# One hand-written order for the attention steps of a fused attention and two-stage MoE kernel

## The chip, the cores and the metric

The kernel runs on one core of a Trainium2 chip. TensorE (PE) multiplies, VectorE (DVE) and ScalarE (ACT) work element by element, GpSimd (POOL) fills constants, and the sync engine's queue (SP) issues nearly all DMAs; ACT's queue issues the rest. Matmul results go to eight PSUM banks. The metric is the device time of one execution, in microseconds; of several runs the median counts.

## The reference

Linear attention without a softmax, an RMS norm over each head, then two feed-forward stages, all in fp32:

```python
kv  = einsum('bhsd,bhse->bhde', k, v)          # b=4, h=8, s=576, d=64
out = einsum('bhsd,bhde->bhse', q, kv)
x   = out / sqrt(mean(out*out, -1) + 1e-6) * g_norm      # -> [2304, 512]
h   = x @ w_in;  x = (h * clip(h + 3, 0, 6) / 6) @ w_out # d_ff = 2048
p   = domain_probs / (domain_probs.sum(-1) + 1e-9)
y   = sum_e p[:, e] * (relu(x @ w1[e]) @ w2[e])          # 4 experts, 1024 wide
```

## The kernel before

**Attention** is done in eight half batches i (a batch, four of its eight heads). For each: `att_q` transposes q on PE into banks `pq` and `kvp` by matmuls with an identity, and ACT copies them out as `qT` (L225 from `pq`, L227 from `kvp`); `att_kv` sums k-transposed times v into `kvp`, and ACT copies the 64x64 blocks into the block-diagonal `kvbd` (L242); `att_out` multiplies `qT` with `kvbd` into three banks `po`, called groups 0, 1 and 2 (2 is half size), whose squares ACT writes to `xt` (L261) and DVE sums (`ssq`, L264); `att_rms` makes 1/rms in small DVE steps around an ACT square root (L287) and scales `po` into `xt` (L277); `att_x` transposes `xt` on PE into three banks `px` (two long pieces 0 and 1, a short piece 2), from which ACT writes `xh` (L323) and DVE the rest `xl` (L324). Each pair `xh`, `xl` holds one fp32 value as two parts that TensorE takes at its faster format.

**Weights** are split in the same way: `convert` turns a raw tile, in two halves, by some ACT steps (L149, L150, L165) and seven DVE steps (L152 to L167) into `w`. `conv(k)` runs k of its pieces.

**The first MoE** works in units u of feature tiles f, over five token blocks t. `ff_in` is 12 matmuls (L342 to L344) into `ph` and an epilogue on ACT and DVE (L348 to L351); `ff_out` is 12 matmuls (L365) into four banks. `step(n)` does `ff_in` of item n, `ff_out` of item n-3 and some conversion. The four items of `EARLY` (unit 0, blocks 0 and 1) have their `ff_in` pulled into the end of attention by `fill`. **The second MoE** (L646, L692) follows and isn't touched.

**The order.** The code is written by loop step: step i issues `att_q`, `att_kv` of i, `att_out` and `att_rms` of i-1 and `att_x` of i-2. A scheduler of the framework then reorders the instructions of all engines by priority and readiness in its own model, so what stands on an engine isn't the order of the code. Each engine runs its own list strictly from the front.

Of the kernel before, what the change touches and what calls it, by code (L numbers as in the profile page):

```python
# [17 lines left out]
def kernel(  # L18
# [63 lines left out]
    psb = ctx.enter_context(tc.tile_pool(name="psb", bufs=5, space=bass.MemoryType.PSUM))  # L82
    psc = ctx.enter_context(tc.tile_pool(name="psc", bufs=1, space=bass.MemoryType.PSUM))
# [23 lines left out]
    ssq = const.tile([P, 5, HH], F32, name="ssq")  # L107
    xH = [(xp0 if t < 3 else xp).tile([P, KD, n], F32R, tag=f"xh{t}", name=f"xh{t}") for t, (_, n) in enumerate(BLK)]
# [68 lines left out]
    def att_load(i):  # L177
        b, hf = divmod(i, 2)
        t = {}
        for nm, src in (("q", q), ("k", k), ("v", v)):  # L180
            m = natile[0] % 7
            natile[0] += 1
            pool, tag = (accp, "acc") if m < 5 else (wp, f"w{m - 1}")
            t[nm] = pool.tile([P, NP, CJ, D], F32, tag=tag, name=f"{nm}in")
            nc.sync.dma_start(
                out=t[nm].rearrange("p r j d -> p r (j d)"),
                in_=src[b, hf * HH:(hf + 1) * HH].rearrange("(r x) (s j) d -> (x s) r (j d)", x=2, j=CJ),
            )
# [21 lines left out]

    def att_q(i):

        t = st[i]
# [4 lines left out]
        for j in range(CJ):
            for x in range(2):
                for r in range(NP):  # L220
                    to = pq[r][half[x ^ r], j, :] if j < CB else kvp[r][half[x ^ r], 1, :]
# [4 lines left out]
        for r in range(NP):
            nc.scalar.activation(out=qv[:, r, :, CB], in_=kvp[r][:, 1, :], func=AF.Copy)  # L227

    def att_kv(i):


        t = st[i]
        kvp = t["kvp"]
        for j in range(CJ):
            for x in range(2):
                for r in range(NP):
                    nc.tensor.matmul(  # L237
                        kvp[r][half[x ^ r], 0, :], lhsT=t["k"][half[x], r, j, :], rhs=t["v"][half[x], r, j, :],
                        start=(j == 0), stop=(j == CJ - 1))
        for r in range(NP):  # L240
            for x in range(2):
                nc.scalar.activation(  # L242
                    out=kvbd[i % 2][half[x ^ r], r, half[x]], in_=kvp[r][half[x ^ r], 0, :], func=AF.Copy)

    def att_out(i):
# [3 lines left out]
        t["xt"] = xt = wp.tile([P, 3, 2, HH, D], F32, tag=f"w{2 + i % 2}", name="xt")  # L249
        t["po"] = []  # L250
        for tt in banks(b):
            po = psb.tile([P, 2, NP, P], F32, tag="b", name="po")
            for m, (o, w) in enumerate(tt):
                for r in range(NP):
                    nc.tensor.matmul(  # L255
                        po[:w, m, r, :], lhsT=t["qT"][:, r, o:o + w], rhs=kvbd[i % 2][:, r, :],
                        start=True, stop=True)
            t["po"].append(po)
        for g, tt in enumerate(banks(b)):
            w, nm = tt[0][1], len(tt)  # L260
            nc.scalar.activation(  # L261
                out=xt[:w, g, :nm].rearrange("p m h d -> p m (h d)"),
                in_=t["po"][g][:w, :nm].rearrange("p m r e -> p m (r e)"), func=AF.Square)
            nc.vector.tensor_reduce(  # L264
                out=ssq[:w, 2 * g:2 * g + nm, :], in_=xt[:w, g, :nm], axis=AX.X, op=ALU.add)

    def att_rms(i):


        b, hf = divmod(i, 2)  # L270
        t = st[i]
        va, r0, w1_, ri = (sp.tile([P, 5, HH], F32, tag=n, name=n) for n in ("va", "r0", "nw", "ri"))

        def scale():
            for g, tt in enumerate(banks(b)):
                w, nm = tt[0][1], len(tt)
                nc.vector.tensor_tensor(  # L277
                    out=t["xt"][:w, g, :nm].rearrange("p m h d -> p (m h) d"),
                    in0=t["po"][g][:w, :nm].rearrange("p m r (h d) -> p (m r h) d", d=D),
                    in1=ri[:w, 2 * g:2 * g + nm, :].rearrange("p m h -> p (m h)").unsqueeze(2).to_broadcast(  # L280
                        [w, nm * HH, D]),
                    op=ALU.mult)

        return [
            lambda: nc.vector.tensor_scalar(
                out=va, in0=ssq, scalar1=1.0 / D, scalar2=1e-6, op0=ALU.mult, op1=ALU.add),
            lambda: nc.scalar.activation(out=r0, in_=va, func=AF.Sqrt),  # L287
            lambda: nc.vector.reciprocal(out=r0, in_=r0),
            lambda: nc.vector.scalar_tensor_tensor(
                out=w1_, in0=va, scalar=FMAX, in1=r0, op0=ALU.min, op1=ALU.mult),  # L290
            lambda: nc.vector.tensor_tensor(out=w1_, in0=w1_, in1=r0, op=ALU.mult),
            lambda: nc.vector.tensor_scalar(
                out=w1_, in0=w1_, scalar1=-0.5, scalar2=1.5, op0=ALU.mult, op1=ALU.add),
            lambda: nc.vector.tensor_tensor(out=ri, in0=w1_, in1=r0, op=ALU.mult),
            scale,
        ]

    def att_x(i):

        b, hf = divmod(i, 2)  # L300
        t = st.pop(i)
        where = {o: (g, m, w) for g, tt in enumerate(banks(b)) for m, (o, w) in enumerate(tt)}
        c = cut(b)
        long, short = ((0, c), (c, S)) if c > S - c else ((c, S), (0, c))
        em = []

        def bank(rs, o0, o1):
            px = bank_a([P, len(rs), o1 - o0], "px")
            for y, r in enumerate(rs):
                for o in sorted(where):  # L310
                    g, m, w = where[o]
                    if o0 <= o < o1:
                        nc.tensor.transpose(  # L313
                            px[:, y, o - o0:o - o0 + w],
                            t["xt"][:w, g, m, 2 * r:2 * r + 2, :].rearrange("p h d -> p (h d)"),
                            ident[:w, :w])
            blk, off = divmod(b * S + o0, TB)
            assert off + o1 - o0 <= BLK[blk][1]
            d = hf * NP + rs[0]
            hi = xH[blk][:, d:d + len(rs), off:off + o1 - o0]  # L320
            lo = xL[blk][:, d:d + len(rs), off:off + o1 - o0]
            em.append((
                lambda: nc.scalar.activation(out=hi, in_=px, func=AF.Copy, scale=gcol[:, 0:1]),  # L323
                lambda: nc.vector.scalar_tensor_tensor(  # L324
                    out=lo, in0=px, scalar=gcol[:, 0:1], in1=hi.bitcast(F32), op0=ALU.mult, op1=ALU.subtract)))

        for r in range(NP):
            bank([r], *long)
        bank(list(range(NP)), *short)
        return em  # L330
# [56 lines left out]
    nearly = [0]  # L387

    def fill():
        ff_in(*EARLY[nearly[0]])  # L390
        nearly[0] += 1
# [395 lines left out]
```

## Time and profile before

| what | value |
|---|---|
| median of three runs | 1234.98 us (1234.45 to 1235.54) |
| profiled execution: time, span | 1236.37 us, 1234.6 us |
| PE busy, share of the span | 1216.7 us, 99% |
| DVE, ACT busy | 759.1 us, 529.6 us |
| chain that ended last, share of PE | 96% |
| largest lines in that chain | po L646 32%, po L365 16%, qa and qb L692 14% each |
| DMA over the span | 87.14 MB, 71 GB/s |

The span runs from the first to the last instruction of the profiled execution; its own time holds 1.8 us more around it. A busy share says how long an engine had an instruction in it, not how fast that went. Times in rows are microseconds from the span's start. Matmuls of fp32 operands show two records each.

### The profile page before, as it was taken

How to read it: one execution, taken by the hardware profiler on the slowest of the kernel's cores; microseconds unless marked ns; L12 is line 12 of the kernel's file. 1: busy time of each engine (PE TensorE's matmuls, PEld its weight loads, DVE VectorE, ACT ScalarE, POOL GpSimd, SP SyncE). 2: the span in 40 equal slices, each digit the busy share in tenths (PEclk: the TensorE clock that was granted, in tenths of full speed). 3: DMA queues.
4: the chain of work that ended last, by engine and by line, in shares of the span. 5: the costliest groups of instructions: out<-in, count | busy, mean ns of one | idle time of the engine just before them, and what ended most of it. 6: DMA issues, size and time to landing. Idle time of an engine off the chain costs nothing.

```text
span 1234.6 us, 17429 instructions
## 1 busy us (share of the span) xinstructions
PE 1216.7 (99%) x7069; PEld 1067.9 (87%) x7069; DVE 759.1 (61%) x1457; ACT 529.6 (43%) x1050; POOL 1.6 (0%) x12
## 2 busy tenths in 40 slices
PE   7899999999999999999999999999999999999998
PEld 5778888888888889999999999999999999999997
DVE  6799974794533656565656595656565956565553
ACT  5667742542322433434444454333333534444441
POOL 0000000000000000000000000000000000000000
PEclk8999999999999999999999999999999999999999
DMA  9712320120010002211111131211221321122111
GB/s 337 232 68 86 104 68 1 52 69 1 19 51 1 1 1 69 68 67 65 60 66 64 62 115 67 69 68 68 69 69 69 109 79 69 69 69 68 69 35 52
DMA packets 60832, 87.14 MB, mean 71 GB/s; under 512 B 5200, under 2 KB 37968, under 8 KB 60752
## 3 DMA queue, kind: packets, MB, share of 16 engines
q1 hardware_dynamic: 60592, 86.03, 20.5%
q8 instruction: 55, 0.90, 0.3%
q14 instruction: 25, 0.20, 0.1%
q10 hardware_dynamic: 160, 0.00, 0.0%
HBM read 81.30 MB, written 4.72 MB: 70 GB/s over the span
## 4 chain that ended last, share of the span: by engine, by line
PE 96%; DMA 1%; DVE 1%; ACT 1%; issue 0%; DVEq 0%
PE po L646 32%; PE po L365 16%; PE qa L692 14%; PE qb L692 14%; PE ph L342 5%; PE ph L343 5%; PE ph L344 5%; PE po L255 1%; PE pq L222 1%; DMA qin<-in_q_dram 1%; PE px L313 1%; DMA raw<-in_moe_w_in_dram 1%; PE kvp L237 0%; DVE ssq L264 0%; PE kvp L222 0%
## 5 line engine op out<-in xcount | busy, mean ns | idle before, releaser
L646 PE MATMUL po<-wout,g 128*128 128x512 f32 x1728 | 420.3, 392 | 0.0
L646 PEld LDWEIGHTS po<-wout,g 128*128 128x128 f32 x1728 | 322.2, 188 | 61.7
L692 PE MATMUL qa<-xs,win 128*128 128x384 f32 x1008 | 203.7, 336 | 0.0
L692 PE MATMUL qb<-xs,win 128*128 128x384 f32 x1008 | 203.6, 336 | 0.0
L365 PE MATMUL po<-gH,w 128*128 128x512 f32 (+1 forms) x640 | 194.0, 369 | 0.0
L692 PEld LDWEIGHTS qa<-xs,win 128*128 128x128 f32 x1008 | 179.8, 188 | 5.7
L692 PEld LDWEIGHTS qb<-xs,win 128*128 128x128 f32 x1008 | 179.7, 188 | 5.6
L365 PEld LDWEIGHTS po<-gH,w 128*128 128x128 f32 x640 | 117.0, 188 | 20.1
L342 PE MATMUL ph<-xh,w 128*128 128x512 f32 (+1 forms) x320 | 118.1, 369 | 0.8 <-DVE xl L324 0.8
L349 DVE SCALAR_TENSOR_TENSOR r<-r,ph 128x512 f32<-128x512 f32 (+1 forms) x80 | 50.5, 632 | 111.2 <-ACT r L348 111.1
L365 PE MATMUL po<-gL,w 128*128 128x512 f32 (+1 forms) x320 | 117.8, 368 | 0.0
L343 PE MATMUL ph<-xl,w 128*128 128x512 f32 (+1 forms) x320 | 117.8, 368 | 0.0
L344 PE MATMUL ph<-xh,w 128*128 128x512 f32 (+1 forms) x320 | 117.8, 368 | 0.0
L348 ACT ACTIVATE r<-ph,three 128x512 f32<-128x512 f32 (+1 forms) x80 | 51.4, 643 | 152.4 <-PE ph L344 152.3
L666 DVE SCALAR_TENSOR_TENSOR g<-qa,g 128x384 fp32r<-128x384 f32 x48 | 26.7, 557 | 119.5 <-ACT g L665 118.2
L561 DVE TENSOR_TENSOR wout<-raw,wout 128x512 fp32r<-128x512 f32 x96 | 65.8, 687 | 28.0 <-ACT wout L560 28.0
L666 DVE SCALAR_TENSOR_TENSOR g<-qb,g 128x384 fp32r<-128x384 f32 x48 | 26.7, 557 | 89.0 <-ACT g L665 89.0
L665 ACT ACTIVATE g<-cs 128x384 fp32r<-128x384 f32 x96 | 49.7, 518 | 56.5 <-DVE cs L713 53.4
L342 PEld LDWEIGHTS ph<-xh,w 128*128 128x128 f32 x320 | 60.3, 188 | 11.5 <-DVE xl L324 1.1
L560 ACT ACTIVATE wout<-raw 128x512 fp32r<-128x512 f32 x96 | 55.4, 624 | 33.5 <-PE po L646 33.5
L344 PEld LDWEIGHTS ph<-xh,w 128*128 128x128 f32 x320 | 60.3, 188 | 10.2
L343 PEld LDWEIGHTS ph<-xl,w 128*128 128x128 f32 x320 | 60.4, 189 | 10.0
(93 smaller groups left out, 1256.8 us busy)
## 6 DMA issues: line engine op xcount, KB each, us to landing
raw<-in_moe_w_dram SPq DMA_DIRECT2D x96, 512.0 KB, 4.2
raw<-in_moe_w_in_dram SPq DMA_DIRECT2D x16, 512.0 KB, 3.7
raw<-in_moe_w_out_dram SPq DMA_DIRECT2D x16, 512.0 KB, 3.6
qin<-in_q_dram SPq DMA_DIRECT2D x8, 576.0 KB, 8.0
kin<-in_k_dram SPq DMA_DIRECT2D x8, 576.0 KB, 6.0
vin<-in_v_dram SPq DMA_DIRECT2D x8, 576.0 KB, 6.3
out_dram<-acc SPq DMA_DIRECT2D x18, 256.0 KB, 2.0
dp<-in_moe_domain_probs_dram SPq DMA_DIRECT2D x1, 36.0 KB, 6.0
```

The source lines that it names most:

```text
L342: nc.tensor.matmul(ph, lhsT=w[:, 0, c, :], rhs=xH[t][:, c, :], start=(c == 0), stop=False)
L343: nc.tensor.matmul(ph, lhsT=w[:, 0, c, :], rhs=xL[t][:, c, :], start=False, stop=False)
L344: nc.tensor.matmul(ph, lhsT=w[:, 1, c, :], rhs=xH[t][:, c, :], start=False, stop=(c == KD - 1))
L348: nc.scalar.activation(out=r, in_=ph, func=AF.Relu, bias=three[:, 0:1])
L349: nc.vector.scalar_tensor_tensor(out=r, in0=r, scalar=6.0, in1=ph, op0=ALU.min, op1=ALU.mult)
L365: nc.tensor.matmul(po_t[u, t][o], lhsT=lhsT, rhs=rhs, start=(f == 0 and m == 0), stop=(f == UF[u] - 1 and m == 2))
L560: nc.scalar.activation(out=dst[0], in_=src, func=AF.Copy)
L561: nc.vector.tensor_tensor(out=dst[1], in0=src, in1=dst[0].bitcast(F32), op=ALU.subtract)
L646: nc.tensor.matmul(ps[i], lhsT=lhsT, rhs=w[:, f, y], start=(j == 0 and f == 0 and m == 0), stop=(j == FP - 1 and f == 1 and m == 2))
L665: nc.scalar.activation(out=g[0], in_=src, func=AF.Relu)
L666: nc.vector.scalar_tensor_tensor(out=g[1], in0=src, scalar=0.0, in1=g[0].bitcast(F32), op0=ALU.max, op1=ALU.subtract)
L692: nc.tensor.matmul(bank, lhsT=w[:, wy, AOP[m], c], rhs=xs[m][:, xy, c], start=first and n == 0, stop=n == 5, skip_group_check=True)
```

## The change

Attention's work is cut into small functions (`q`, `qc`, `kv`, `kvc`, `out`, `sq`, `ssq`, `rt`, `va`, `nw`, `sc`, `x`, `hi`, `lo`), and a table `STEPS` names for each loop step which of them comes when and for which half batch (its second entry is the lag). `tc.manual_schedule()` takes the scheduler out for this part: each engine gets its instructions in the order of the table. A table `ELSE` places conversions, raw loads, the early `ff_in` items (now three pieces: matmuls, first and second half of the epilogue) and the expert probabilities at (loop step, place). `kvp`, `pq`, `px` and the early `ph` rotate over five banks instead of three, `po` over three. The square root takes `ssq` itself, with scale and bias, and the Newton step is one DVE instruction shorter. The gain vector and the probabilities are loaded at the start from ACT's queue; the loads of k and v of half batch i+2 and of q of i+3 are issued from SP's queue right behind the k-v sum of i.

```diff
-    psb = ctx.enter_context(tc.tile_pool(name="psb", bufs=5, space=bass.MemoryType.PSUM))
-    psc = ctx.enter_context(tc.tile_pool(name="psc", bufs=1, space=bass.MemoryType.PSUM))
+    psb = ctx.enter_context(tc.tile_pool(name="psb", bufs=3, space=bass.MemoryType.PSUM))
+    psc = ctx.enter_context(tc.tile_pool(name="psc", bufs=3, space=bass.MemoryType.PSUM))
...
     def bank_a(shape, name):
+        pool, tag = (psa, "a") if turn["a"] % 5 < 2 else (psc, "c")
         turn["a"] += 1
-        pool, tag = (psc, "c") if turn["a"] % 3 == 0 else (psa, "a")
...
+    def att_rt(i):
+        st[i]["r0"] = r0 = sp.tile([P, 5, HH], F32, tag="r0", name="r0")
+        nc.scalar.activation(out=r0, in_=ssq, func=AF.Sqrt, scale=1.0 / D, bias=eps[:, 0:1])
...
-    load_raw()
-    att_load(0)
-    load_raw()
-    load_raw()
...
-    att_load(1)
-    conv(6)
+    STEPS = (
+        ("kvc", 1), ("out", 1, 1), ("out", 1, 0), ("x", 2, 0), ("sq", 1, 1), ("out", 1, 2), ("sq", 1, 0),
+        ("lo", 3, 2), ("hi", 2, 0), ("sq", 1, 2), ("x", 2, 1), ("ssq", 1, 1), ("ssq", 1, 0), ("lo", 2, 0),
+        ("hi", 2, 1), ("q", 0), ("qc", 0), ("ssq", 1, 2), ("lo", 2, 1), ("rt", 1), ("kv", 0), ("va", 1),
+        ("nw", 1), ("sc", 1, 1), ("x", 2, 2), ("sc", 1, 0), ("sc", 1, 2), ("hi", 2, 2))
...
+    n = len(STEPS)
+    ELSE = {
+        (1, n): lambda: conv(3), (3, n): lambda: conv(1), (5, n): load_raw, (6, 20): lambda: conv(1),
+        (7, n): lambda: (fill(0), conv(2)),
+        (8, 9): lambda: (fill(1), fill(0)), (8, 16): lambda: conv(2), (8, 19): lambda: fill(0),
+        (8, n): lambda: (fill(2), fill(1), load_raw(), conv(2)),
+        (9, 11): lambda: fill(1), (9, 14): lambda: conv(2),
+        (9, n): lambda: (fill(3), load_raw(), fill(2), fill(2)),
+        (10, n): lambda: (fill(3), fill(3), probabilities()),
+    }
-    for i in range(NHB + 2):
-        if 1 <= i < NHB - 1:
-            att_load(i + 1)
-        if i >= NHB - 1:
-            load_raw()
-        if i == 4:
-            nc.sync.dma_start(out=dp, in_=moe2_domain_probs.rearrange("(t p) e -> p t e", p=P))
-        if i < NHB:
-            att_q(i)
-            if i == 0:
-                warm(4)
-            att_kv(i)
-        conv({0: 6, 1: 13}.get(i, 0))
...
+    with tc.manual_schedule():
...
+        nc.scalar.dma_start(out=dp, in_=moe2_domain_probs.rearrange("(t p) e -> p t e", p=P))
+        load_raw()
+        att_load(0, "q")
+        load_raw()
+        for x in ((0, "k"), (0, "v"), (1, "q"), (1, "k"), (1, "v")):
+            att_load(*x)
+        load_raw()
+        att_load(2, "q")
+
+        conv(10)
+        for i in range(NHB + 3):
+            for m, (name, lag, *part) in enumerate(STEPS):
+                if (i, m) in ELSE:
+                    ELSE[i, m]()
+                if 0 <= i - lag < NHB:
+                    DO[name](i - lag, *part)
+                if name == "kv":
+                    for x in ((i + 2, "k"), (i + 2, "v"), (i + 3, "q")):
+                        att_load(*x)
+                    if i == 0:
+                        warm(4)
+            if (i, n) in ELSE:
+                ELSE[i, n]()
+        ahead[0] = True
+        for n in range(FIRST):
+            step(n)
```

What this does to the lists of the engines, at three places. First PE in one loop step in the middle of attention, before and then changed; `pq`, `kvp` are the transposes of q and the k-v sum, `po` the product, `px` the transposes of the result.

```order
L255 MATMUL po<-kvbd_110,qT 128x128 x5
L222 MATMUL pq<-ident,qin 64x64 x32
L222 MATMUL kvp<-ident,qin 64x64 x2
L255 MATMUL po<-kvbd_110,qT 128x128 x2
L222 MATMUL kvp<-ident,qin 64x64 x2
L255 MATMUL po<-kvbd_110,qT 128x128
L237 MATMUL kvp<-vin,kin 64x64 x36
L255 MATMUL po<-kvbd_110,qT 64x128 x2
```

```order
L262 MATMUL po<-kvbd_110,qT 128x128 x8
L320 MATMUL px<-ident,xt 128x128 x3
L320 MATMUL px<-ident,xt 128x64
L262 MATMUL po<-kvbd_110,qT 64x128 x2
L320 MATMUL px<-ident,xt 128x128 x3
L320 MATMUL px<-ident,xt 128x64
L223 MATMUL pq<-ident,qin 64x64 x32
L223 MATMUL kvp<-ident,qin 64x64 x4
L243 MATMUL kvp<-vin,kin 64x64 x36
L320 MATMUL px<-ident,xt 128x128 x2
```

Before, products of the half batch ahead stand between the transposes of q and the k-v sum; now the k-v sum follows the transposes directly, and the products stand at the head of the step.

Second ACT in the same part, before and then changed; `xh` is what ACT writes from `px`.

```order
L225 ACTIVATE qT<-pq 128x64x8 x2
L227 ACTIVATE qT<-kvp 128x64 x2
L261 ACTIVATE xt<-po 128x512
L149 ACTIVATE x<-raw 128x512
L242 ACTIVATE kvbd_110<-kvp 64x64 x4
L261 ACTIVATE xt<-po 64x256
L323 ACTIVATE xh_115<-px,gcol 128x384 x2
```

```order
L232 ACTIVATE qT<-pq 128x64x8 x2
L234 ACTIVATE qT<-kvp 128x64 x2
L282 ACTIVATE r_930<-ssq,eps 128x20
L331 ACTIVATE xh_116<-px,gcol 128x2x128
L250 ACTIVATE kvbd_111<-kvp 64x64 x4
L269 ACTIVATE xt<-po 128x512 x2
L331 ACTIVATE xh_116<-px,gcol 128x384
```

The copy of the short piece (`xh_116`, 2x128) now stands ahead of the `kvbd` copies, and the conversion step (`x<-raw`) is gone from this place.

Third ACT in the changed kernel after the last half batch's products; `w` is a converted weight half, `gH` the early items' result.

```order
L269 ACTIVATE xt<-po 64x256
L331 ACTIVATE xh_117<-px,gcol 128x320
L166 ACTIVATE w<-r 128x512
L359 ACTIVATE gH<-r 128x512
L282 ACTIVATE r_1341<-ssq,eps 128x20
L331 ACTIVATE xh_118<-px,gcol 128x512
```

The weight half of feature tile 1 and the last square root stand here behind a copy from `px`; in the kernel before, that weight half is converted far ahead of this place.

## Rows read from the trace of the kernel before

**Rows 1.** Busy time by stretch; columns in its first line.

```profile
core 0: us, PE busy (x) PEld busy (x) DVE busy (x) ACT busy (x) POOL busy (x), PEclk, DMA share, GB/s
0.00:6.00 6.00, 4.82 (x12) 1.60 (x12) 1.07 (x3) 2.79 (x4) 1.62 (x12) 1.00 0.66 231
6.00:24.00 18.00, 11.05 (x305) 9.69 (x304) 11.63 (x22) 10.65 (x25) 0.00 (x0) 0.72 1.00 381
24.00:76.00 52.00, 46.91 (x1039) 39.15 (x1038) 44.37 (x116) 33.66 (x96) 0.00 (x0) 0.97 0.64 209
76.00:99.25 23.25, 22.43 (x117) 17.38 (x115) 20.37 (x48) 15.87 (x34) 0.00 (x0) 1.00 0.15 46
99.25:1234.60 1135.35, 1131.51 (x5604) 1000.11 (x5602) 681.67 (x1271) 466.60 (x896) 0.00 (x0) 1.00 0.18 59
```

**Rows 2.** Timeline of ACT and PE: start, us, engine, line, operation.

```profile
23.97 0.77 ACT L242 ACTIVATE kvbd<-kvp 64x64 f32<-64x64 f32 x4
...
39.61 0.79 ACT L242 ACTIVATE kvbd<-kvp 64x64 f32<-64x64 f32 x4 [1.04 <-PE kvp L237]
...
75.87 0.79 ACT L242 ACTIVATE kvbd<-kvp 64x64 f32<-64x64 f32 x4 [0.62 <-PE kvp L237]
...
99.25 0.40 PE L342 MATMUL ph<-xh,w 128*128 128x512 f32 x1
...
107.15 2.72 PE po L365 x12
```

**Rows 3.** Timeline, transposes of q, copies and k-v sum, PE and ACT.

```profile
24.78 1.16 PE L222 MATMUL pq<-ident,qin 64*64 64x64 f32 x64
...
26.00 1.08 ACT L225 ACTIVATE qT<-pq 128x512 f32<-128x512 f32 x2 [0.50 <-PE kvp L222]
...
66.12 0.41 ACT L227 ACTIVATE qT<-kvp 128x64 f32<-128x64 f32 x2
...
66.46 1.39 PE L237 MATMUL kvp<-vin,kin 64*64 64x64 f32 x72 [0.33 <-ACT qT L227]
...
67.89 0.79 ACT L242 ACTIVATE kvbd<-kvp 64x64 f32<-64x64 f32 x4 [0.36 <-PE kvp L237]
```

**Rows 4.** Timeline, transposes of the result, products, ACT held by a raw load, and kvbd.

```profile
39.86 1.36 PE L313 MATMUL px<-ident,xt 128*128 128x128 f32 x10
...
41.14 1.38 PE L255 MATMUL po<-kvbd,qT 128*128 128x128 f32 x10
...
50.15 0.66 ACT L149 ACTIVATE x<-raw 128x512 f32<-128x512 f32 x1 [3.44 <-DMA raw<-in_moe_w_in_dram]
...
51.27 0.78 ACT L242 ACTIVATE kvbd<-kvp 64x64 f32<-64x64 f32 x4
...
51.76 1.12 PE L313 MATMUL px<-ident,xt 128*128 128x128 f32 x6 [1.87 <-ACT kvbd L242]
```

**Rows 5.** Groups by line, first 100 us, ACT and DVE.

```profile
L323 ACT ACTIVATE xh<-px,gcol 128x384 fp32r<-128x384 f32 x6 | 3.3, 580 | 0.0
...
L323 ACT ACTIVATE xh<-px,gcol 128x128 fp32r<-128x128 f32 x2 | 0.7, 365 | 0.0
...
L277 DVE TENSOR_TENSOR xt<-po,ri 128x512 f32<-128x512 f32 x16 | 10.4, 684 | 0.2
```

**Rows 6.** Timeline at the start: ACT's conversion steps, PE's warming matmuls.

```profile
1.18 4.92 PE L450 MATMUL zp<-zero 128*128 128x512 bf16 x12 [1.18 <-DVE zero L445]
...
4.47 0.66 ACT L149 ACTIVATE x<-raw 128x512 f32<-128x512 f32 x1 [2.46 <-DMA raw<-in_moe_w_in_dram]
...
8.79 0.63 ACT L165 ACTIVATE w<-r 128x512 fp32r<-128x512 f32 x1 [1.58 <-DVE r L163]
```

**Rows 7.** Busy time by stretch, columns as in the first group.

```profile
50.00:55.00 5.00, 3.24 (x28) 2.79 (x30) 3.78 (x9) 4.45 (x13) 0.00 (x0) 0.84 1.04 395
...
55.00:60.00 5.00, 4.97 (x146) 4.46 (x143) 4.97 (x14) 3.02 (x8) 0.00 (x0) 0.82 0.49 147
```

**Rows 8.** Timeline of SP, the load behind that of the probabilities.

```profile
40.58 4.59 SPq L185 DMA_DIRECT2D qin<-in_q_dram  x1
```

**Rows 9.** Groups by line, 100 to 160 us, DVE.

```profile
L167 DVE TENSOR_TENSOR w<-r,w 128x512 fp32r<-128x512 f32 x12 | 8.2, 685 | 0.0
```

More of the change, by code (lines that the diff above doesn't have):

```diff
@@ L242, in att_kv, with att_out @@
                 nc.scalar.activation(
-                    out=kvbd[i % 2][half[x ^ r], r, half[x]], in_=kvp[r][half[x ^ r], 0, :], func=AF.Copy)
-    def att_out(i):
+                    out=kvbd[i % 2][half[x ^ r], r, half[x]], in_=st[i]["kvp"][r][half[x ^ r], 0, :], func=AF.Copy)
+    def att_out(i, g):
+        t = st[i]
+        if "po" not in t:
+            t["xt"] = wp.tile([P, 3, 2, HH, D], F32, tag=f"w{2 + i % 2}", name="xt")
+            t["po"] = {}
+        t["po"][g] = po = psb.tile([P, 2, NP, P], F32, tag="b", name="po")
+        for m, (o, w) in enumerate(banks(i // 2)[g]):
+            for r in range(NP):
+                nc.tensor.matmul(
+                    po[:w, m, r, :], lhsT=t["qT"][:, r, o:o + w], rhs=kvbd[i % 2][:, r, :],
+                    start=True, stop=True)
@@ L248, in att_out @@
         t = st[i]
[L249 to L302, printed above, removed]
         c = cut(b)
         long, short = ((0, c), (c, S)) if c > S - c else ((c, S), (0, c))
[L305 to L330, printed above, removed]
@@ new lines, in att_x @@
+        rs, (o0, o1) = ([y], long) if y < NP else (list(range(NP)), short)
+        px = bank_a([P, len(rs), o1 - o0], "px")
+        for z, r in enumerate(rs):
+            for o, g, m, w in sorted((o, g, m, w) for g, tt in enumerate(banks(b)) for m, (o, w) in enumerate(tt)):
+                if o0 <= o < o1:
+                    nc.tensor.transpose(
+                        px[:, z, o - o0:o - o0 + w],
+                        t["xt"][:w, g, m, 2 * r:2 * r + 2, :].rearrange("p h d -> p (h d)"),
+                        ident[:w, :w])
@@ L335, with ff_in @@
     po_t = {}
-    def ff_in(u, t, f):
+    def ff_in(u, t, f, bank=None):
         n = BLK[t][1]
         w = W[u, f][:, 0].rearrange("p j (c f) -> p j c f", c=KD)
-        ph = psa.tile([P, TB], F32, tag="a", name="ph")[:, :n]
+        ph = (bank([P, TB], "ph") if bank else psa.tile([P, TB], F32, tag="a", name="ph"))[:, :n]
         for c in range(KD):
@@ L386 @@
     EARLY = [(0, t, f) for f in range(UF[0]) for t in range(2)]
[L387 to L391, printed above, removed]
+    FIRST = 4
+    early_in = [ff_in(*x, bank=bank_a) for x in EARLY]
     def step(n):
         if n < NI and items[n] not in EARLY:
-            ff_in(*items[n])
+            for _ in ff_in(*items[n]):
+                pass
         if n >= LAG:
@@ L497, with fill, probabilities @@
-    ahead[0] = True
-    while nearly[0] < len(EARLY):
-        fill()
+    STEPS = (
+        ("kvc", 1), ("out", 1, 1), ("out", 1, 0), ("x", 2, 0), ("sq", 1, 1), ("out", 1, 2), ("sq", 1, 0),
[3 rows of a table added]
+    DO = dict(q=att_q, qc=att_qc, kv=att_kv, kvc=att_kvc, out=att_out, sq=att_sq, ssq=att_ssq, rt=att_rt,
+              va=att_va, nw=att_nw, sc=att_sc, x=att_x, hi=att_hi, lo=att_lo)
+    def fill(k):
+        next(early_in[k])
+    def probabilities():
+        nc.vector.tensor_reduce(out=psum_e, in_=dp, axis=AX.X, op=ALU.add)
+        nc.vector.tensor_scalar(out=psum_e, in0=psum_e, scalar1=1e-9, scalar2=None, op0=ALU.add)
+        nc.vector.reciprocal(out=psum_e, in_=psum_e)
+        nc.vector.tensor_scalar(out=psum_e, in0=psum_e, scalar1=1.0 / 6.0, scalar2=None, op0=ALU.mult)
+        nc.vector.tensor_tensor(
+            out=prob, in0=dp, in1=psum_e.unsqueeze(2).to_broadcast([P, NTT, E]), op=ALU.mult)
```

122 lines of the change are left out of this document (77 added, 45 removed).

## The prediction

> **What bounds the kernel now.** I read first the busy time by stretch [rows 1]. From 99.25 us, where the first `ff_in` behind attention starts [rows 2], to the end PE is busy 1131.5 of 1135.35 us: it bounds that part, and the change leaves its matmuls there as they are. What the change can win or lose lies ahead of 99.25: PE is idle 1.2 us of the first 6, 6.9 of the next 18, 5.1 of the 52 from 24 to 76, and 0.8 of the last 23. So the whole stake is about 14 us, half of it in the first 24. Then I read the timeline for the loop's own clock, the `kvbd` copies on ACT, which each half batch passes once: the second stands at 23.97, the fourth at 39.61, the eighth and last at 75.87 [rows 2]. Six steps, from the second copy to the last, take 51.9 us. One of them, from 39.61 to 51.27 [rows 2, 4], takes 11.66, because two conversion steps stand ahead of `kvbd` on ACT and wait 3.44 us for a raw load [rows 4]; the other five average (51.9 - 11.66)/5 = 8.05. I cut the change at the second `kvbd` and at the last one, and cost three pieces: start, six steps, tail. The matmuls of attention are nearly the same in number, so the cost of the new order is the sum of what each engine waits for.
>
> **The start, -1.7 us.** The chain that begins it is ACT's conversion. The first half's `w` is written at 8.79 for 0.63 [rows 6], and the loads that feed it keep their place; in the new list the next raw tile's two steps follow it (0.66 by the first of them, overlapping, 1.25 for both), then `qT`(0) at 10.65. `kv` starts when `qT` is copied: 1.08 for the pair from `pq`, and from the start of the pair from `kvp` 0.34 more, 66.12 to 66.46, so 1.43 in all [rows 3]; `kvbd` 1.43 later (66.46 to 67.89), at 13.5. Four warming matmuls stand now behind the k-v sum of 0, at 4.92/12 = 0.41 each [rows 6]: 15.0 before the first products. These are 20 records at 1.38/10 [rows 4], 2.7 us, at half clock 5.4; I take 3.2, so 18.2. `q`(1) to `qT` is 1.22 (24.78 to 26.00), `kv` 1.43 later and `kvbd`(1) 1.43 after that [rows 3]: 22.3 against 23.97 [rows 2]. Bounds: the products all cold +2.2, all warm -0.5. The loads of probabilities and gain on ACT's queue no longer stand ahead of a load of q, which in the trace was 4.59 us behind the probabilities [rows 8]; they run now while q, k and v of 0 and 1 are in flight, with the start at 381 GB/s [rows 1]. The trace has no row of them there. By the nearest row they cost from nothing to about half of 4.59, and I take nothing for the sum, since DMA moves 231 to 381 GB/s there either way. The Trainium skill, "DMA: Bandwidth & Descriptors", section "Issuing engines are not separate DMA queues", says that transfers started from different engines end up on the same 16 DMA engines; no run here shows it. By that rule the move frees SP's queue but not the transfers, and the start would come out at up to +0.6 instead of -1.7 (an estimate from the same 4.59).
>
> **The six steps, +3.3 us.** What stands between two `kvbd` in the new list. PE starts 0.49 after `kvbd` does (51.27 to 51.76, [rows 4]); 16 product records, 2.2; a long piece of `xt`'s transposes, 3 or 4 at 0.136 [rows 4], 0.5; the four short products, 0.55; the other long piece, 0.5: `q` begins at about 4.3. `qT` follows after 1.22, `kv` after another 1.43 [rows 3]. In these 1.43 PE has nothing to do: before, products of the half batch ahead stood there (the wait then was 0.33, [rows 3]); now the transposes of q stand directly ahead of `kv`. `kv` takes 1.39 [rows 3], the short piece 0.3 to 0.5. On ACT its copy `xh` now stands ahead of `kvbd`: 0.365 [rows 5], more for the wider ones (0.58). So 4.3 + 1.22 + 1.43 + 1.39 + 0.3 + 0.37 = 9.0 us for a step. PE waits for 1.43 and about 1.0 in each. Squares, `ssq`, square root, Newton and scaling (three `sc`, 0.684 for a long one, [rows 5]) lie beside PE's `q` and `kv`: what hides them is the wait just named, and if they came late the short transposes would wait, which stand ahead of nothing but `xh` and `kvbd`, so that `kvbd` slips by the same amount. In one step a conversion (1.2 on ACT, two steps as in [rows 4]) stands ahead of `kvbd`. Six steps: 6 x 9.0 + 1.2 = 55.2, against 51.9: +3.3. Bounds 8.5 to 9.5 for a step, the first if `xh` is hidden and transposes overlap as they do in part in the trace, the second if DVE delays the short piece: 0.3 to 6.3. Taking the conversions off ACT's place ahead of `kvbd` is what gives back the 3.4 us stall [rows 4]; that is in the sum, as the 9.0 stands against an average with the stall in it (8.65).
>
> **The tail, -0.7 us.** From `kvbd`(7) to 99.25 there were 23.4 us [rows 2]; then 15 `ff_out` matmuls stood ahead of that `ff_in`, in the new list 12, at 2.72/12 each [rows 2], so like with like is 22.7. Behind the new `kvbd`(7) PE has four early `ff_in` of 2.72 (the price of twelve such matmuls, [rows 2]), 10.9, products 2.7, transposes of two half batches 2.6, twelve `ff_out` 2.72, less 0.8 by which the first early `ff_in` starts ahead of `kvbd`: 18.1. Three waits come on top: I estimate 1.0 where the third early `ff_in` waits for the weight half of feature tile 1, which now stands behind a copy from `px` on ACT; 1.6 where the last transposes wait for the last scaling, whose chain (sum, square root, Newton, 0.684 for a scaling [rows 5]) stands behind two subtractions of other work on DVE; and 1.1 where the fourth waits for a bank. 22.0 - 22.7 = -0.7, between -2 and +1.
>
> **Sum.** -1.7 + 3.3 - 0.7 = +0.9 us on a profiled execution of 1236.37, so 1237.2. That one lies 1.4 us above the median of the runs, 1234.98; the forecast for the median is 1235.8. About 0.2%, 2.5 us, is what a measurement of this kernel can tell from no change.
>
> **The rivals.** *The clock falls in the new waits: slower.* After a wait of 1.87 us for `kvbd` [rows 4] the granted clock read 0.84 and 0.82 in the ten microseconds that follow [rows 7], so somewhere in there PE ran at 1.2 GHz for about (0.16 + 0.18) x 5/0.5 = 3.4 us, and lost some 1.7. The new order has two waits of 1.0 to 1.43 in each of six steps. Against it: from 24 to 76 the mean clock was 0.97 with waits of 5.1 us in all [rows 1]. Two more falls than before, at 1.7 each, give 1239.2; from the second on this case decides. The Trainium skill, "TensorE: Matmul & The Clock Gate", section "Why this matters for your kernels", warns only of idle gaps longer than any of these; by it no step would lose clock and the sum stands, while the trace shows a fall behind a gap of 1.87 us, so the page does not rule this rival out.
>
> *Conversions come late: slower.* The new table places fewer weight halves in attention, and more are left for the first `ff_in` behind it. In the 60 us from 100 twelve halves were converted [rows 9], 5.0 us each, and the last of the seven DVE steps of each took 0.685. If the feature tiles are wanted at one per five `ff_in` plus `ff_out`, 5 x 5.4 = 27 us, two halves for each tile fit, but the first ones are short of slack; PE would wait 0 to 5 us near item 10 to 14. Middle 3.5: 1239.3.
>
> *Shorter steps: faster.* If the transposes and copies hide better than I count, and a step comes near 8.35, which is nearer to the five undisturbed steps of before (8.05) than to my 9.0, the six take 6 x 8.35 + 1.2 = 51.3, -0.6 instead of +3.3: 1231.9. For it speaks that the new order frees SP's and ACT's lists from the raw loads; against it, the two waits named above.
>
> **How the numbers follow.** Forecast, 1235.8 with 1233.3 to 1238.3 for its own range: 0.38. Clock 0.17, late conversions 0.12, shorter steps or a shorter tail 0.33. The forecast's own spread leaves its band a little on both sides; I count that with the others. Faster by over 0.2% (below 1232.5): 0.33; within: 0.37; slower (above 1237.5): 0.30. The range for 8 in 10 reaches to the shorter steps less a shorter tail (1230.2) and to a fall of the clock together with the upper bound of a step (1240).
>
> **What would show it.** `kvbd`(0) at 13.5 and `kvbd`(1) at 22.3: the start. A pitch of 9.0 us between `kvbd` from the second to the last, PE waiting 1.4 us at the k-v sum for ACT's copy from `kvp` and 1.0 at the products for `kvbd`: the steps; a pitch of 8.4 or less says the rival. A granted clock below 1.00 between 24 and 76 in more than one place: the clock. 22 us from the last `kvbd` to the first `ff_in` of the third block, with three waits: the tail. PE idle behind 100 us on a weight half: late conversions. The prediction fails most easily in the pitch: 0.4 us a step is 2.4 us.

## The result, and the profile after

The changed kernel takes 1249.3 us (median; 1248.35 to 1249.95) against 1235.15 for the kernel before on the same chips: 1.0115 times, interval 1.0097 to 1.0132, so some 14 us slower. Forecast was 1235.8, range 1230.2 to 1240. The profiled execution has a span of 1248.1 us, 13.5 more than the one of before. Two executions that took far longer than the others of their kernel, one of the kernel before (1336.73 us) and one of e9_order_pad64 (2433.64 us), are left out of all medians and ratios here.

First the busy time by stretch, stretches and columns those of [rows 1].

```profile
0.00:6.00 6.00, 3.59 (x8) 1.04 (x8) 0.59 (x2) 2.49 (x4) 1.64 (x13) 1.00 0.66 221
6.00:24.00 18.00, 11.94 (x315) 10.24 (x316) 11.12 (x24) 8.32 (x25) 0.00 (x0) 0.98 0.83 265
24.00:76.00 52.00, 39.93 (x875) 34.27 (x875) 31.07 (x74) 27.64 (x77) 0.00 (x0) 0.88 0.62 209
76.00:99.25 23.25, 20.30 (x243) 15.59 (x241) 15.74 (x36) 12.08 (x29) 0.00 (x0) 1.00 0.07 24
99.25:1248.10 1148.85, 1144.53 (x5635) 1006.97 (x5634) 704.66 (x1316) 477.01 (x916) 0.00 (x0) 1.00 0.18 61
```

Against [rows 1], the first 24 us have about as much idle PE, 8.5 us for 8.1. From 24 to 76 PE is busy 39.93 us and not 46.91, at a mean clock of 0.88 and not 0.97. The last line looks as in the kernel before, PE busy nearly throughout; what is wrong there a busy share can't show.

The loop's own clock, the `kvbd` copies on ACT in the timeline, answers to [rows 2]:

```profile
22.74 0.81 ACT L250 ACTIVATE kvbd<-kvp 64x64 f32<-64x64 f32 x4 [0.71 <-PE kvp L243]
...
33.27 0.80 ACT L250 ACTIVATE kvbd<-kvp 64x64 f32<-64x64 f32 x4
...
44.51 0.80 ACT L250 ACTIVATE kvbd<-kvp 64x64 f32<-64x64 f32 x4
...
56.13 0.80 ACT L250 ACTIVATE kvbd<-kvp 64x64 f32<-64x64 f32 x4
...
65.28 0.80 ACT L250 ACTIVATE kvbd<-kvp 64x64 f32<-64x64 f32 x4
...
84.10 0.80 ACT L250 ACTIVATE kvbd<-kvp 64x64 f32<-64x64 f32 x4
```

The second copy stands at 22.74 (before 23.97), the last at 84.10 (75.87). The first three of the six steps take 10.5, 11.2 and 11.6 us, the other three 9.3 on average. Then the first `ff_in` of the third block, and the second MoE's first matmul, PE in the timeline, of after:

```profile
106.32 0.40 PE L349 MATMUL ph<-xh,w 128*128 128x512 f32 x1
```

```profile
491.32 0.34 PE L726 MATMUL qb<-xs,win 128*128 128x384 f32 x1
```

and the second MoE's start of before:

```profile
475.56 0.34 PE L700 MATMUL qb<-xs,win 128*128 128x384 f32 x1
```

With these marks the spans come apart into five pieces (us; for the tail and the first MoE, 0.68 is taken off the 99.25 of [rows 2] for the three matmuls by which the lists differ there, as the prediction does):

| piece | before | after | difference | forecast |
|---|---|---|---|---|
| to the second `kvbd` | 23.97 | 22.74 | -1.2 | -1.7 |
| six steps | 51.9 | 61.4 | +9.5 | +3.3 |
| last `kvbd` to the third block's `ff_in` | 22.7 | 22.2 | -0.5 | -0.7 |
| from there to the second MoE | 377.0 | 385.0 | +8.0 | 0 |
| second MoE and end | 759.0 | 756.8 | -2.2 | 0 |

Start and tail came within 0.5 us of what was worked out. The steps cost three times what was said, and the first MoE, which the change leaves alone, costs 8 us more.

**The steps.** One step without a slow clock, PE in the timeline:

```profile
65.78 2.18 PE L262 MATMUL po<-kvbd,qT 128*128 128x128 f32 x16 [0.91 <-ACT kvbd L250]
67.80 0.49 PE L320 MATMUL px<-ident,xt 128*128 128x128 f32 x3
...
68.80 0.55 PE L320 MATMUL px<-ident,xt 128*128 128x128 f32 x3
69.28 1.16 PE L223 MATMUL pq<-ident,qin 64*64 64x64 f32 x64
...
71.86 1.39 PE L243 MATMUL kvp<-vin,kin 64*64 64x64 f32 x72 [1.31 <-ACT qT L234]
73.18 0.99 PE L320 MATMUL px<-ident,xt 128*128 128x128 f32 x4
75.19 1.06 PE L262 MATMUL po<-kvbd,qT 128*128 128x128 f32 x6 [1.01 <-ACT kvbd L250]
```

It is the chain that was summed: products, transposes, `q` 4.0 after `kvbd` (69.28, 65.28), 1.31 idle ahead of the k-v sum, 1.01 ahead of the next products. The pitch is 9.4 where 9.0 was forecast (74.69 against 65.28; the later row stands with e11_hi_late below). In the first three steps the clock is another (busy time by stretch):

```profile
24.00:28.00 4.00, 4.00 (x24) 3.66 (x23) 1.79 (x4) 1.55 (x3) 0.00 (x0) 0.66 1.03 391
...
32.00:36.00 4.00, 3.20 (x47) 2.90 (x39) 2.11 (x6) 1.07 (x6) 0.00 (x0) 0.69 0.89 332
...
44.00:48.00 4.00, 2.99 (x14) 2.99 (x15) 0.70 (x3) 1.86 (x7) 0.00 (x0) 0.50 0.88 256
48.00:52.00 4.00, 4.00 (x56) 2.99 (x59) 2.28 (x4) 2.13 (x4) 0.00 (x0) 0.67 0.09 35
```

The granted clock is 0.66 and 0.69 in two of these stretches, and 0.50, all of it at 1.2 GHz, in a third that runs on into the next; between them it is back at 1.00 (28 to 32) and 0.97 (40 to 44): three falls. PE's waits of the whole run, by who ended them (us in total, times, the longest):

```profile
PE kvp L243 <- ACT qT L234: 12.7, 8, 3.6
PE po L262 <- ACT kvbd L250: 6.2, 6, 1.9
...
PE px L320 <- DVE xt L302: 1.1, 1, 1.1
PE ph L349 <- ACT w L166: 0.5, 1, 0.5
PE ph L349 <- DVE xl L335: 0.5, 1, 0.5
```

The two waits of a step lead: 12.7 us over eight half batches for `qT`, 6.2 over six for `kvbd`.

**The first MoE.** The chain that ended last counts twelve `ff_out` matmuls as 2.80 us, where [rows 2] has 2.72:

```profile
120.48 2.80 PE po L375 x12
```

That is 233.3 ns for a matmul of 512 columns and not 226.7, at a granted clock of 1.00 and with nothing waited for. At 24 matmuls an item takes 5.60 us and not 5.44. 377.0 x 5.60/5.44 would be 388; items of the block of 256 columns, which are not slowed (twelve take 1.40 us, before 1.43), bring it near the 385 measured.

### The profile page after: what moved, and what is told of

The parts are those of the page before. It is cut to its first block, busy times and chain, and to the rows that moved or that the text cites. A ratio compares the mean times of both kernels' runs of the same rounds, so it can differ in the third digit from the quotient of the medians.

```text
span 1248.1 us, 17411 instructions
## 1 busy us (share of the span) xinstructions
PE 1220.3 (98%) x7069; PEld 1068.1 (86%) x7069; DVE 763.2 (61%) x1449; ACT 527.6 (42%) x1049; POOL 1.6 (0%) x13
## 4 chain that ended last, share of the span: by engine, by line
PE 97%; ACT 2%; DVE 1%; DMA 0%; issue 0%; DVEq 0%
PE po L672 31%; PE po L375 16%; PE qa L718 14%; PE qb L718 14%; PE ph L349 5%; PE ph L350 5%; PE ph L351 5%; PE po L262 2%; PE kvp L243 1%; PE px L320 1%; ACT qT L232 1%; PE pq L223 1%; DMA raw<-in_moe_w_in_dram 0%; ACT xh L331 0%; ACT kvbd L250 0%
## 5 line engine op out<-in xcount | busy, mean ns | idle before, releaser
L672 PE MATMUL po<-wout,g 128*128 128x512 f32 x1728 | 415.3, 389 | 0.0
L349 PE MATMUL ph<-xh,w 128*128 128x512 f32 (+1 forms) x320 | 119.4, 373 | 1.1 <-ACT w L166 0.5
L351 PE MATMUL ph<-xh,w 128*128 128x512 f32 (+1 forms) x320 | 119.1, 372 | 0.0
L349 PEld LDWEIGHTS ph<-xh,w 128*128 128x128 f32 x320 | 60.0, 188 | 13.5 <-ACT w L166 0.8
L375 PEld LDWEIGHTS po<-gL,w 128*128 128x128 f32 x320 | 60.0, 188 | 11.6
```

The source lines that it names most:

```text
L375: nc.tensor.matmul(po_t[u, t][o], lhsT=lhsT, rhs=rhs, start=(f == 0 and m == 0), stop=(f == UF[u] - 1 and m == 2))
L672: nc.tensor.matmul(ps[i], lhsT=lhsT, rhs=w[:, f, y], start=(j == 0 and f == 0 and m == 0), stop=(j == FP - 1 and f == 1 and m == 2))
```

## The experiments

All times are medians against the kernel before on the same chip, 1235.2 to 1235.7 there; a ratio has its interval where there are several runs.

**Banks, e1_banks.** The change sizes two PSUM pools anew, and so the results go to other banks.

```diff
-    psb = ...(name="psb", bufs=3)
-    psc = ...(name="psc", bufs=3)
+    psc = ...(name="psc", bufs=3)
+    psb = ...(name="psb", bufs=3)
```

> Where 6 to 9 us went behind attention: in the changed kernel an item of the first MoE (24 matmuls) takes 5.60 us, in the kernel before 5.44, with PE busy throughout in both. Theory banks: the pitch hangs on which PSUM banks the results go to. This kernel gives the two pools whose sizes were changed each other's bank numbers and leaves everything else; by this theory the item comes to about 5.44 us and the run to about 1240. By the other theories (count of instructions ahead, addresses in SBUF, a phase at entry) the pitch stays at 5.60 and the run near 1249.

1251.27 us in one run; twelve `ff_out` matmuls take 2.80 us as in the changed kernel. Exchanging the banks changes nothing; e5_pad below, with the changed kernel's banks and 2.72, settles that it isn't the banks.

**Place in the list, e2_count.**

```diff
+    nc.tensor.matmul(zp[:64, :64], lhsT=ident[:64, :64], rhs=ident[:64, :64], start=True, stop=True)
     for x in kvbd:
```

> Theory count: the pitch hangs on where in PE's list of instructions the stream of matmuls stands. One small fp32 matmul on the identity is added at the start, while PE waits for the first load; it adds an odd number of instructions ahead of everything and no time. By this theory the item of the first MoE leaves 5.60 us for 5.44 and the run comes to about 1240; by banks, SBUF addresses or a phase at entry that each entry finds anew it stays at 5.60 and 1249.

1247.74 us in one run, twelve matmuls again 2.80. Not the count of instructions.

**Addresses, first try, e3_sbuf.**

```diff
+    shift = const.tile([P, 16], F32, name="shift")
+    nc.gpsimd.memset(shift, 0.0)
     ident = const.tile([P, P], F32, name="ident")
```

> Theory addresses: the pitch hangs on the addresses of the operands in SBUF. A constant tile of 64 bytes per partition is put ahead of the others and moves every tile of the left side by 64 bytes. By this theory the item of the first MoE may leave 5.60 us for 5.44, with the run at about 1240; by the other theories nothing changes, 5.60 and 1249.

1255.38 us in one run. The item stayed at 5.60, as the other theories said, but the second MoE took 761.4 us and not 756.8, which none of them gave: addresses matter for something. The allocation list of the built programs showed what. The change itself adds a small tile among the constants, for the square root's bias:

```diff
     ssq = const.tile([P, 5, HH], F32, name="ssq")
+    eps = const.tile([P, 1], F32, name="eps")
```

`eps` takes 32 bytes, and all tiles of SBUF's left side that come behind it move by 32: the results of the activation, `gH`, from 46080 to 46112, `xh0` from 91136 to 91168, and so on. The first MoE's converted weights `w` lie on the right side and don't move. In e3_sbuf the shift is 96 (and the constants ahead of `eps` move by 64). A pad of 48 words ahead of these tiles makes their start a multiple of 1024 in the kernel before.

**The offset taken back, e5_pad**, and **given to the kernel before, e6_before_pad**; no other edit.

```diff
-    PADL, PADR = 48, 248
+    PADL, PADR = 40, 248
```

```diff
-    PADL, PADR = 48, 248
+    PADL, PADR = 56, 248
```

> Theory offset: the small tile of the square root's bias, put among the constants, moves every tile of SBUF's left side (x, its two parts, the results of the activation) by 32 bytes, and matmuls that stream from there are slower at that offset; a shift by 64 bytes more left the item at 5.60 us. This kernel is the changed one with 32 bytes taken off the pad ahead of those tiles, so that they stand where they stood before. By this theory an item of the first MoE takes 5.44 us again, the second MoE loses the 2 to 3 us that it gained, and the run comes to 1241.5 to 1244. By the rival, that the order of the instructions or the banks sets it, the item stays at 5.60 and the run at 1249.

> The same theory from the other side: the kernel before with 32 bytes more in that pad, and nothing else. By theory offset its item of the first MoE rises from 5.44 to 5.60 us, the second MoE gains 2 to 3 us, and the run is 5.5 to 7.5 us longer, 1240.5 to 1242.5, with attention as it was. By the rival it stays within 1 us of 1235.

e5_pad 1241.1 us, 1.0050 (1.0034 to 1.0067); e6_before_pad 1242.64 us, 1.0058 (1.0043 to 1.0073); both lie just outside the expected ranges, by 0.4 and 0.1. The chain that ended last of e5_pad, and of e6_before_pad:

```profile
110.54 2.72 PE po L375 x12
```

```profile
107.70 2.80 PE po L365 x12
```

With the offset taken back the changed kernel has the 2.72 of [rows 2] again; with it the old kernel has 2.80. The second MoE follows too: 759.0 in e5_pad, 756.8 in e6_before_pad, the two values of the table above, crossed. Attention of e6_before_pad ends as before (99.61). In e5_pad, whose median is 8.2 below the changed kernel's, attention also ended 4.1 earlier in the profile (the third block's `ff_in` at 102.21), with the long steps shorter (more of it under e4_fill); e6_before_pad has the offset alone: 6.3 by the spans, 7.1 by the medians. Every profiled run with a shift of 32, whatever its order, has 2.80 (also e1, e2, e4, e11), and every one with none has 2.72 in most items (also e7). So it is an address, not an order.

**Another offset, e8_pad64** (pad 56 in the changed kernel: 64 bytes from the place before) and **e10_before_pad64** (pad 64 in the kernel before).

> The changed kernel with the left side moved by 64 bytes against the kernel before, where 32 and 96 gave 5.60 us an item. If what counts is whether the tiles start at a multiple of 64 bytes, the item takes 5.44 and the run 1241 to 1244; if any offset from the place before costs, it stays at 5.60 and 1249.

> The kernel before with 64 bytes more in the pad, nothing else. Theory offset: attention as before, the first MoE slower by 1 to 2 us, the second faster by 7.5 to 8: 1228 to 1230.5. If the offset of 64 bytes helps only with the changed banks or order, it stays at 1235.

Neither end of the first expectation: e8_pad64 took 1234.73 us in one run, 14.6 below the changed kernel and level with the kernel before. Chain of e8_pad64:

```profile
107.57 2.75 PE po L375 x12
```

```profile
700.92 1.04 PE qb L718 x6
701.96 3.19 PE po L672 x14
```

and of the kernel before, in the same stretch:

```profile
705.37 1.07 PE qa L692 x6
...
707.48 3.22 PE po L646 x14
```

Twelve matmuls take 2.75, between the two values; in the second MoE six matmuls of 384 columns take 1.04 nearly always and not 1.04 to 1.07, fourteen of 512 3.19 for 3.22. The second MoE comes to 751.5 us, 7.5 less than before. In the kernel before the same offset gave 1229.44 us, 0.9954 (0.9937 to 0.9971), in the expected range; the first MoE cost only 0.5 more, not 1 to 2. By offset, from the starts of the second MoE and the spans:

| shift of the left side, bytes | 12 `ff_out` | second MoE to the end |
|---|---|---|
| 0 (before, e5_pad) | 2.72 | 759.0, 759.0 |
| 32 (after, e6_before_pad) | 2.80 | 756.8, 756.8 |
| 64 (e8_pad64, e10_before_pad64) | 2.75, 2.75 | 751.5, 751.5 |
| 96 (e3_sbuf) | 2.80 | 761.4 |

**The clock, e4_fill.** Zeros are multiplied into the products' bank while PE waits for `kvbd`.

```diff
+        for _ in range(4 if g == 1 and i else 0):
+            nc.tensor.matmul(
+                po.rearrange("p m r e -> p (m r e)"), lhsT=zero[:, :P], rhs=zero, start=True, stop=True)
         for m, (o, w) in enumerate(banks(i // 2)[g]):
```

> Theory clock: three of the six steps take 10.4 to 11.6 us and not 9.3, because the granted clock falls in the waits of PE. Four matmuls on zeros are put ahead of the products of each half batch from the second on, into the bank that the products overwrite, so that PE works while it waits for kvbd (about 0.9 of the wait). By this theory the clock stays at 1.00 from 24 to 76 us, all steps take 9.2 to 9.6, and the run is 4 to 6 us shorter, 1243 to 1245. By the rival, that the long steps come from late conversions or loads, the three steps stay long and the run is as before or up to 2 us longer. Eight instructions more per half batch also move the stream, so the pitch of the first MoE is read apart.

1245.76 us, 1.0086 (1.0065 to 1.0106), 3.5 less than the changed kernel's 1249.3 (measured apart), where 4 to 6 were expected. Busy time by stretch, and the last `kvbd`, in e4_fill:

```profile
24.00:76.00 52.00, 42.33 (x994) 34.38 (x1001) 33.02 (x80) 31.55 (x87) 0.00 (x0) 1.00 0.61 210
```

```profile
21.99 0.81 ACT L250 ACTIVATE kvbd<-kvp 64x64 f32<-64x64 f32 x4 [0.72 <-PE kvp L243]
...
31.44 0.80 ACT L250 ACTIVATE kvbd<-kvp 64x64 f32<-64x64 f32 x4
...
41.41 0.79 ACT L250 ACTIVATE kvbd<-kvp 64x64 f32<-64x64 f32 x4
...
78.52 0.80 ACT L250 ACTIVATE kvbd<-kvp 64x64 f32<-64x64 f32 x4
```

The clock is 1.00 throughout, the six steps take 56.5 us and not 61.4, and the long steps are gone but for the one of 10.0, which holds the conversion. At the end of that step PE waited 1.90 us for `kvbd` in the changed kernel; in e4_fill zeros stand in the wait, with 0.27 left ahead of them and 0.62 behind:

```profile
45.01 3.78 PE L262 MATMUL po<-kvbd,qT 128*128 128x128 f32 x16 [1.90 <-ACT kvbd L250]
```

```profile
41.90 2.18 PE L265 MATMUL po<-kvbd,qT 128*128 128x128 f32 x16 [0.62 <-ACT kvbd L250]
```

The same step table without zeros ran in five more profiles, e1_banks, e2_count, e3_sbuf, e5_pad and e8_pad64. With the changed kernel's own, all six have the wait of 1.9 and a clock below 1.00 behind it (0.79 to 0.89 from 40 to 56). From 24 to 40, behind waits of 0.7 to 1.3, three of them read 0.79 to 0.81 and three 1.00, and from 56 to 76, with waits of 0.9 to 1.3, all read 1.00. So how many falls come is not fixed by the table. The mildest of the six is e5_pad, with the second and the last `kvbd`:

```profile
24.00:76.00 52.00, 39.64 (x962) 33.38 (x960) 33.16 (x78) 30.19 (x82) 0.00 (x0) 0.97 0.60 201
```

```profile
22.37 0.81 ACT L250 ACTIVATE kvbd<-kvp 64x64 f32<-64x64 f32 x4 [0.71 <-PE kvp L243]
...
80.19 0.80 ACT L250 ACTIVATE kvbd<-kvp 64x64 f32<-64x64 f32 x4
```

Its six steps take 57.8 us. Against the 56.5 of e4_fill the falls cost 1.3 us there and 4.9 in the changed kernel's profile. That they come from the waits rests on one profile with zeros against six without, and on 3.5 us in the medians; a wait need not bring one: in e10_before_pad64 PE waited 2.84 us for `kvbd` and the clock stayed at 1.00 behind it.

**One copy moved, e11_hi_late.** ACT copies the short piece behind `kvbd`, not ahead of it; the later places of `ELSE` move by one.

```diff
-        ("kvc", 1), ("out", 1, 1), ...
+        ("kvc", 1), ("hi", 3, 2), ("out", 1, 1), ...
...
-        ("nw", 1), ("sc", 1, 1), ("x", 2, 2), ("sc", 1, 0), ("sc", 1, 2), ("hi", 2, 2))
+        ("nw", 1), ("sc", 1, 1), ("x", 2, 2), ("sc", 1, 0), ("sc", 1, 2))
```

> The changed kernel with one move: ACT copies the short piece from px behind the kvbd copies and not ahead of them. The prediction put 0.37 us of each step on this copy. By that, the pitch of kvbd in the steps without a fall of the clock goes from 9.3 to 8.8 to 9.0, PE's wait for kvbd from 0.9 to about 0.5, and the run is 2.5 to 4 us shorter than the changed kernel's 1249.3; up to 6 more if the shorter wait also keeps the clock up. If the copy was hidden, pitch and time stay.

1241.44 us, 1.0051 (1.0037 to 1.0066): 7.9 us less than the changed kernel's 1249.3, inside what was expected if the clock stays up. In its trace it is 1.00 from 24 to 76:

```profile
24.00:76.00 52.00, 42.15 (x1049) 35.65 (x1050) 37.52 (x90) 33.45 (x95) 0.00 (x0) 1.00 0.62 206
```

```profile
57.93 0.81 ACT L250 ACTIVATE kvbd<-kvp 64x64 f32<-64x64 f32 x4 [1.29 <-PE kvp L243]
...
66.01 0.81 ACT L250 ACTIVATE kvbd<-kvp 64x64 f32<-64x64 f32 x4 [1.29 <-PE kvp L243]
```

The pitch fell to 8.1 to 8.5 in all but the first of the six steps (9.1), by about 1.0 and not by 0.37. In the changed kernel's ACT list the copy did not only take its own time:

```profile
74.21 0.58 ACT L331 ACTIVATE xh<-px,gcol 128x384 fp32r<-128x384 f32 x1 [2.15 <-PE px L320]
74.69 0.45 ACT L250 ACTIVATE kvbd<-kvp 64x64 f32<-64x64 f32 x2
```

ACT stands idle 2.15 us, until the short transposes are there, and `kvbd` behind it: 74.69 is 2.83 after the k-v sum began (71.86). In e11_hi_late it is 66.01 - 64.53 = 1.48. So the short transposes and the copy held `kvbd` for 1.35 us, where the sum had 0.3 and 0.37: the term was the wait of the copy, not the copy.

**The order, e7_order**, with the offset as before (pad 40). Two conversions move from ahead of `kvbd` to behind it; the other entries of `ELSE` stand at the matching places.

```diff
+        ("kvc", 1), ("out", 1, 1), ("out", 1, 0), ("hi", 3, 1), ("hi", 3, 2), ("sq", 1, 1), ("lo", 3, 1),
+        ("sq", 1, 0), ("lo", 3, 2), ("q", 0), ("qc", 0), ("ssq", 1, 1), ("x", 2, 0), ("out", 1, 2),
+        ("ssq", 1, 0), ("sq", 1, 2), ("hi", 2, 0), ("ssq", 1, 2), ("rt", 1), ("va", 1), ("kv", 0),
+        ("nw", 1), ("sc", 1, 1), ("lo", 2, 0), ("sc", 1, 0), ("sc", 1, 2), ("x", 2, 1), ("x", 2, 2))
```

> The order of the steps: products of the half batch ahead and a piece of the transposes stand between the transposes of q and the k-v sum, the other two pieces behind the sum, and ACT copies kvbd ahead of two of its copies from px; the offset is as before. Theory order and clock: the two waits of each step go, the pitch of kvbd falls from 9.3 to between 7.2 and 8.2 us, the clock stays at 1.00 from 24 to 76 us, and the run comes to 1225 to 1232, faster than both kernels. Rival: the loads (390 GB/s in the first 36 us) or the conversions become the bound; the pitch stays at 8.5 or more or PE waits for weights behind attention, and the run is at 1232 to 1238.

1228.38 us, 0.9942 (0.9927 to 0.9957): faster than both kernels. In e7_order, PE and ACT:

```profile
58.12 1.16 PE L223 MATMUL pq<-ident,qin 64*64 64x64 f32 x64
...
59.32 0.55 PE L320 MATMUL px<-ident,xt 128*128 128x128 f32 x3
59.80 0.65 PE L262 MATMUL po<-kvbd,qT 128*64 128x128 f32 x4
60.64 1.39 PE L243 MATMUL kvp<-vin,kin 64*64 64x64 f32 x72 [0.19 <-ACT qT L234]
```

```profile
54.31 0.81 ACT L250 ACTIVATE kvbd<-kvp 64x64 f32<-64x64 f32 x4 [0.27 <-PE kvp L243]
...
62.13 0.81 ACT L250 ACTIVATE kvbd<-kvp 64x64 f32<-64x64 f32 x4 [0.44 <-PE kvp L243]
```

A piece of the transposes and the short products now fill the time in which ACT copies `qT`; PE waits 0.19 ahead of the sum and not 1.31. The pitch is 7.8 to 8.1 in four of the six steps, the first takes 10.3 and the second 6.8, and the third block's `ff_in` starts at 91.0. The mean clock from 24 to 76 is 0.98. Order and conversions were changed together; against e5_pad, which has the same offset, they give 12.7 us.

**Order and offset together, e9_order_pad64 and e12_best** (the same kernel).

> The order of e7_order with the offset of e8_pad64 (64 bytes from the place before), nothing else. If order and offset act apart, attention ends as in e7_order (the third block's first ff_in at 91 us), the first MoE loses some 1 us against e7_order and the second wins 7.5 to 8, so 1221 to 1223. If the gain of the offset hangs on the order, less than 3 us of it shows.

> The kernel of e9_order_pad64 again, whose one profiled execution took twice the time of its others and can't be read. Order and offset acting apart: the third block's first ff_in at 91 us as in e7_order, 512-column matmuls at 228.9 ns in the first MoE and 384-column ones at 173.4 ns in the second as in e8_pad64, span about 1220.5, median 1221 to 1224.

1222.97 us and 0.9911 (0.9888 to 0.9935) the first time (1222.35 to 1227.54), 1224.39 us and 0.9904 (0.9887 to 0.9920) the second. The first lies in the expected 1221 to 1223, the second 0.4 above its 1221 to 1224: the two gains add up but for a microsecond or two. In e12_best the third block's `ff_in` starts at 93.7 and not at 91: PE stood 1.87 us inside one k-v sum, for nothing that the profile shows, and the clock read 0.57 from 40 to 44. From 24 to 76:

```profile
24.00:76.00 52.00, 46.66 (x1053) 38.94 (x1053) 36.26 (x88) 32.73 (x92) 0.00 (x0) 0.94 0.60 208
```

The second MoE is the 751.5 of the table. It is the fastest kernel here, some 11 us below the one before.

## Why the prediction was wrong, step by step

**The start, -1.7 against -1.2: right in its sum, in part by luck.** `kvbd`(1) stood at 22.74 where 22.3 was worked out, but `kvbd`(0) at 14.67 and not 13.5: the slow matmuls stood in the first k-v sum (2.25 us, not 1.39), not in the products, which took 2.68 and not 3.2. The first weight half was written at 9.32 and not 8.79, behind a raw load that came 0.5 later; whether the loads of probabilities and gain did that isn't shown, as no run moves them alone.

**The six steps, +3.3 against +9.5: the term was mis-sized.** Two parts. The chain in a step was the right one, with its 1.31 and 1.01 of waiting, at 9.2 to 9.4 for 9.0; without falls it comes to 56.5 us (e4_fill) for the 55.2 of the sum. What was mis-sized in it is the short piece and its copy, put at 0.3 and 0.37, while they held `kvbd` for 1.35 and moving the copy away gave about 1.0. The greater part in this profile is the clock, 4.9 us, which the prediction held as a rival with 0.17: 1.7 for each fall and two more falls than before. It fell three times, and the price was right; e5_pad, with the same table, lost only 1.3. The Trainium skill, "TensorE: Matmul & The Clock Gate", section "Why this matters for your kernels", by which the sum would stand without this term, warns only of idle gaps longer than any of these; here the trace decides, and waits of at most 1.9 us, two in each step, were followed by stretches at 0.50 to 0.69. The forecast chose between row and rule by chances; the row of before, with its single fall behind a wait of 1.87 [rows 4, 7], was the better witness.

**The tail, -0.7 against -0.5: right in its sum, by luck.** Its terms, 18.1 and 1.0, 1.6 and 1.1, add up to 21.8 and -0.9, not 22.0 and -0.7. The three waits were there, but 0.5, 1.1 and 0.5, the last for DVE's `xl` and not for a bank; the matmuls took about as much more as the waits took less.

**"The change leaves its matmuls there as they are": the step that failed.** The matmuls of both MoEs are the same in number, size and order, and PE is as busy; from this the prediction took that this part costs the same, and gave no rival to it. But a 4-byte tile among the constants moved the operands by 32 bytes, and at that offset a 512-column matmul takes 233.3 ns for 226.7 in the first MoE: +8.0, with -2.2 in the second. e5_pad and e6_before_pad show it from both sides, with no other edit. By the pieces that is 5.8 of the 13.5 us, by e6_before_pad's medians 7.1, and no row of the kernel before could have priced it; the pad words in the code could have been a warning.

**Rivals.** Late conversions: no sign of them beyond a wait of 0.5 for a weight. Shorter steps: not with this table; 8.1 to 8.5 with one copy moved (e11_hi_late), 7.8 with another order (e7_order).

**What stays open.** Why an offset of 32 or 96 bytes costs in the first MoE, 64 a little, and why the second MoE ranks them otherwise (64, 32, 0, 96), isn't shown; only shifts of the whole left side were tried, not of one operand alone. Nor is it shown which waits make the clock fall, or why the same ones did in some steps and profiles and not in others: filling one (e4_fill) or shortening it (e11_hi_late) sufficed in one profile each. In e7_order and e12_best the wait for `qT` was 0.2 at most, but waits of 0.7 to 1.6 stood ahead of the products, mostly for DVE's `xt`, and the mean clock from 24 to 76 was 0.98 and 0.94, so it fell there too.

## What to carry to other kernels

Where code around a bound stretch is edited, compare the time of one matmul there before and after, not only PE's busy share, and look whether a new tile has moved the operands; shifting them by a pad of 32 or 64 bytes costs little to try, and 64 gave the kernel before 5.9 us here, near the 7.2 of the best order with the old offset. In an order written by hand, put work of another item between a step and the copy that it waits for, and never put a copy that waits for PE ahead of the one that PE waits for. Short idle waits that repeat can cost the clock on top of their own length, and not by the same amount each time: 1.3 to 4.9 us here with one step table.

## What the runs showed of the hardware that was not expected

The rate of a matmul with PE busy and the granted clock at 1.00 hangs on the operands' place in SBUF: 226.7, 233.3 and 229 ns (2.72, 2.80 and 2.75 us for twelve) for 512 columns in the first MoE at shifts of 0, 32 or 96, and 64 bytes, and a second MoE of 751.5 to 761.4 us by the same shift. And the granted clock read 0.50 from 44 to 48 us, where PE had waited 1.90 us for `kvbd`, and 1.00 at the same place where zeros left 0.27 and 0.62 of that wait (e4_fill).
